# A decode block fed by one stream of transfers: two small arrays join larger transfers, one transfer is merged, one modulation moves

## The chip, the cores and the metric

The kernel runs on one NeuronCore of a Trainium2 chip. The metric is the device time in microseconds (us) of one execution. The engines are TensorE (PE: matmul, PEld: the loading of its stationary operand), VectorE (DVE), ScalarE (ACT), GpSimd (POOL) and SyncE (SP). Transfers between HBM and the on-chip memory run on 16 DMA engines, whichever engine issued them.

## The reference

All arrays are float32. Batch 2, one token, width 512; the attention has 32 heads of 128 with 4096 cached keys and values each.

```python
mod = (silu(c) @ w_mod).reshape(2, 6, 1, -1)
sa, ca, ga, sb, cb, gb = (mod[:, i] for i in range(6))
h = layernorm(x) * (1 + ca) + sa
x = x + ga * attention(h, k_cache, v_cache, wq, wo)   # q = h @ wq, softmax, @ wo
h = layernorm(x) * (1 + cb) + sb
x = x + gb * (mish(h @ w1 + b1) @ w2)                 # w1: 512 x 1376, w2: 1376 x 512
```

The keys and values are 2 x 32 x 4096 x 128 each, 134 MB each, and every byte of them is read once. A modulation is one sixth of `silu(c) @ w_mod`.

## The kernel before

**The stream.** All large inputs are laid out beforehand as rows, one for each of the 128 partitions, and are read in a fixed order that `stream()` writes out: a list of loads, each with one or more transfers. All of them are issued by SP, on one queue, at L143. Load 0 holds the weights of modulations 0 to 2 (`m012`) and the first two blocks of `wq`, in two transfers. Then come the keys and values, head by head, with blocks of `wq` and `wo` attached to some. The last three loads are the last block of `wo` with `m4` and the last head's values; `m3` with `w1` in three transfers (`m3`, the first half of `w1`, the second half); and `m5` with `w2` in five. A load goes to one of three buffers (two of tag "two", one of tag "one"), so it is issued when everything of the load three places earlier has been used (`used`, L148 to L156).

Beside the stream ACT issues three small transfers: `c` and `x` (`head`, eight rows of 512 bytes each, into `cq` and `xq`, L163 to L165) and the biases `b1c` (128 rows of 48 bytes into `bias`, L167).

**The head of the kernel.** PE turns `c` into columns (L250); silu gives `ct`. Then come the mean and the variance of the first norm (L204, L212), a matmul that puts the biases into `fps` (L263), modulations 0 to 2 (L241 under L265), the first two projections to queries (L288), all in this order on PE.

**The heads.** For each head DVE multiplies the keys by the query (L316) and sums over the 128 columns (L319); the softmax runs on ACT, and PE sums the values with the weights of an earlier head (L365).

**The tail.** After the last values, PE finishes the attention output (L403). `centred` (L194 to L213) computes mean and variance of the new `x`: PE's two matmuls (L204, L212) stand between DVE steps, and `more_work` is put between them. Modulation 3 is computed in two halves, one ahead of the mean and one ahead of the variance. Its result is used at L510, when the second norm is formed. Then follow `w1` (L521), the columns of the hidden layer on top of the biases (L536), modulation 5, mish, `w2` (L561), and the output. `busy(n)` (L293) runs matmuls whose result nobody reads, at places where PE would be idle.

Of the kernel before, what the change touches and what calls it, by code (L numbers as in the profile page):

```python
# [8 lines left out]
F32 = mybir.dt.float32  # L9
# [4 lines left out]
P = 128  # L14
WIDTHS = (384, 384, 352, 256)
# [4 lines left out]
W = 2048  # L20
SIZES = {
    "k": BIG, "v": BIG, "wq": W, "wo": W, "m012": 3 * W, "m3": W, "m4": W, "m5": W,
    "w1": 4 * sum(WIDTHS), "w2": 512 * len(CHUNKS),
}
AHEAD = (14, 22)

# [1 line left out]
def stream():  # L28

    behind, pieces = {}, [("k", 0)]
    for h in range(1, HEADS):
        pieces.append(("k", h))
        if h not in AHEAD:
            behind[h] = len(behind)
            pieces.append(("v", behind[h]))
    left = list(range(len(behind), HEADS))
    pieces += [("v", h) for h in left[:-1]]

    extra = {}
    for c in range(2, HEADS // HC):
        at = (pieces.index(("k", HC * c)) - 1) // 5 * 5
        extra[at] = [("wq", c), ("wo", c - 2)]
    extra[60] = [("wo", HEADS // HC - 2)]
    loads = [[([("m012", 0), ("wq", 0), ("wq", 1)], (3 * W, 2 * W))]]
    n = 0
    while n < len(pieces):
        m = 1 if n % 5 == 0 else 2
        keys = pieces[n : n + m]  # L50
        if keys[0] == ("v", left[0]) and m == 2:
            loads.append([([key], (BIG,)) for key in keys])
        else:
            keys = keys + (extra.pop(n, []) if m == 1 else [])
            loads.append([(keys, (sum(SIZES[kind] for kind, _ in keys),))])
        n += m
    assert not extra and len(loads) % 3 == 0
    last = HEADS - 1
    loads += [
        [([("wo", HEADS // HC - 1), ("m4", 0)], (2 * W,)), ([("v", last)], (BIG // 2, BIG // 4, BIG // 4))],  # L60
        [([("m3", 0), ("w1", 0)], (W, 2 * sum(WIDTHS), 2 * sum(WIDTHS)))],
        [([("m5", 0), ("w2", 0)], (W, 6 * 512, 3 * 512, 512, 512))],
    ]
    return loads, behind, left
# [3 lines left out]
def kernel(  # L68
# [1 line left out]
    tc: tile.TileContext,  # L70
    loads: list,
    head: bass.AP,
    b1c: bass.AP,
    behind: dict,
    left: list,
    out: bass.AP,
# [44 lines left out]
    def take(t, keys):  # L121
        lo = 0
        for kind, n in keys:
            part = t[:, lo : lo + SIZES[kind]]
            lo += SIZES[kind]
            if kind in "kv":
                (k_t if kind == "k" else v_t)[n] = part.rearrange("p (b j d) -> p b j d", b=B, d=DH)
            elif kind in ("wq", "wo"):
                (wq_t if kind == "wq" else wo_t)[n] = part.rearrange("p (k n) -> p k n", k=G)
            else:  # L130
                w_t[kind] = part.rearrange("p (k n) -> p k n", k=NCH if kind == "w2" else G)

    w_t = {}
    done = set()
# [13 lines left out]
    def used(*keys):  # L148

        nonlocal loaded  # L150
        done.update(keys)
        while loaded < len(loads) and (
            loaded < 3 or all(key in done for keys, _ in loads[loaded - 3] for key in keys)
        ):
            load(loaded)
            loaded += 1  # L156
# [1 line left out]
    used()  # L158


    cq = work.tile([P, P], F32, tag="xn", name="cq", bufs=1)
    xq = const.tile([P, P], F32, name="xq")
    for t, src in ((cq, head[0]), (xq, head[1])):  # L163
        nc.gpsimd.memset(t, 0.0)
        nc.scalar.dma_start(out=t[::TB, :], in_=src)  # L165
    bias = const.tile([P, NCH + 1], F32, name="bias")
    nc.scalar.dma_start(out=bias, in_=b1c)  # L167
    nc.scalar.preload_act_table_set("natural_log_exp_and_others")
    ident = const.tile([P, P], F32, name="ident")
    make_identity(nc, ident)  # L170
# [23 lines left out]
    def centred(src, name, first_sum=None, between=None):  # L194

        rs = const.tile([P, 8], F32, name=f"rs_{name}")
        xc = work.tile([P, P], F32, tag="xc", name=f"xc_{name}", bufs=1)
        sq = work.tile([P, P], F32, tag="sq", name=f"sq_{name}", bufs=1)
        if first_sum is None:
            nc.vector.tensor_reduce(out=rs[:, 0:1], in_=src, axis=AX.X, op=ALU.add)  # L200
        else:
            first_sum(rs[:, 0:1])
        mps = small_ps(f"mean_{name}")
        nc.tensor.matmul(mps[:, 0:1], lhsT=mean_w, rhs=rs[:, 0:1], start=True, stop=True)  # L204
        nc.vector.tensor_scalar(out=xc, in0=src, scalar1=mps[:, 0:1], scalar2=None, op0=ALU.subtract)
        nc.vector.scalar_tensor_tensor(
            sq, xc, 1.0, xc, op0=ALU.mult, op1=ALU.mult, accum_out=rs[:, 1:2]
        )
        if between is not None:
            between()  # L210
        vps = small_ps(f"var_{name}")
        nc.tensor.matmul(vps[:, 0:1], lhsT=mean_w, rhs=rs[:, 1:2], start=True, stop=True)  # L212
        return xc, vps[:, 0:1], rs  # L213
# [20 lines left out]
    def modulation(name, n, t, ps=None, ks=range(G)):  # L234


        if ps is None:
            ps = wide_ps(f"modps{name}")[:, : n * P].rearrange("p (m n) -> p m n", m=n)
        for k in ks:
            for g in range(G):  # L240
                nc.tensor.matmul(  # L241
                    ps[R * g : R * (g + 1)],
                    lhsT=ct[:, k, :],
                    rhs=t[:, k, :].rearrange("p (m n) -> p m n", m=n)[:, :, P * g : P * (g + 1)],
                    start=(k == 0),
                    stop=(k == G - 1),
                )
        return ps
# [11 lines left out]
    nc.vector.tensor_scalar(out=xn, in0=xc, scalar1=y0, scalar2=y1, op0=ALU.mult, op1=ALU.mult)  # L260

    fps = psum.tile([P, 512], F32, tag="att2", name="fps", bufs=1)[:, : NJ * G * B]
    nc.tensor.matmul(fps, lhsT=ident, rhs=bias[:, :, None].to_broadcast([P, NJ * G, B]), start=True, stop=False, skip_group_check=True)  # L263

    ps = modulation("0", 3, w_t["m012"])  # L265
    hq = const.tile([P, P], F32, name="hq")
# [1 line left out]
    nc.vector.tensor_tensor(out=hq, in0=ps[:, 0, :], in1=hq, op=ALU.add)  # L268
    mod = {}

    def keep(m, ps):
        mod[m] = const.tile([P, P], F32, name=f"mod{m}")
        nc.scalar.copy(mod[m], ps)

    keep(2, ps[:, 2, :])
    hps = columns(hq, "hps")
    hc = const.tile([P, G, B], F32, name="hc")
    nc.vector.tensor_copy(hc, hps)  # L278
# [14 lines left out]
    def busy(n):  # L293

        for lo in range(0, n, 2):
            cols = P * min(2, n - lo)
            nc.tensor.matmul(ov[1][:, :cols], lhsT=ident, rhs=e_t[0][0].rearrange("p c m -> p (c m)")[:, :cols], start=True, stop=True)
# [130 lines left out]

    project_q(0)
    project_q(1)  # L430
    used(("m012", 0), ("wq", 0), ("wq", 1))
    for h in range(H):
        products(h)
        if h:
# [61 lines left out]
    def add_x(total):  # L496
        nc.vector.scalar_tensor_tensor(x2, xg, 1.0, xq, op0=ALU.mult, op1=ALU.add, accum_out=total)

    mps3 = modulation("3", 1, wm3, ks=(0, 1))

    def more_work():
        modulation("3", 1, wm3, mps3, (2, 3))
        busy(1)

    xc, var, rs = centred(x2, "b", add_x, more_work)
    busy(6)
    nc.vector.tensor_tensor(out=m4, in0=xc, in1=m4, op=ALU.mult)
    y0, y1 = rstd(var, rs)
    nc.scalar.activation(xc, m4, AF.Copy, scale=y0)
# [37 lines left out]

    nc.vector.tensor_scalar(out=f[:, 0], in0=hid, scalar1=30.0, scalar2=None, op0=ALU.min)
    nc.scalar.activation(f[:, 0], f[:, 0], AF.Exp)
    keep(5, gps[:, 0, :])  # L550
    busy(6)
    nc.vector.scalar_tensor_tensor(f[:, 1], f[:, 0], 2.0, f[:, 0], op0=ALU.add, op1=ALU.mult)
    nc.vector.tensor_scalar(out=f[:, 2], in0=f[:, 1], scalar1=2.0, scalar2=None, op0=ALU.add)
# [20 lines left out]
def _lay_out(np, a):  # L574


    def rows(w):

        return w.reshape(-1, P, w.shape[-1]).transpose(1, 0, 2)

    def q_rows(v):

        return v.reshape(2, 4, P).transpose(1, 0, 2).reshape(8, P)

    B, H, S, DH = a["A_k_cache"].shape
    kv = {
        kind: a[n].reshape(B, H, P, -1).transpose(1, 2, 0, 3).reshape(H, P, -1)
        for kind, n in (("k", "A_k_cache"), ("v", "A_v_cache"))
    }
    wq = rows(a["A_wq"]).reshape(P, 4, 8, 512).transpose(2, 0, 1, 3).reshape(8, P, -1)  # L590
    wo = a["A_wo"].reshape(8, 4, P, 512).transpose(0, 2, 1, 3).reshape(8, P, -1)
    wm = rows(a["w_mod"])
    w1 = rows(a["B_w1"])
    starts = np.cumsum((0,) + WIDTHS)
    b1c = np.zeros((P, 12), a["B_b1"].dtype)
    w2 = np.zeros((P, len(CHUNKS), 512), a["B_w2"].dtype)
    for n, (g, j) in enumerate(CHUNKS):
        f0 = starts[g] + P * j
        f1 = min(f0 + P, starts[g + 1])
        b1c[: f1 - f0, n] = a["B_b1"][f0:f1]  # L600
        w2[: f1 - f0, n] = a["B_w2"][f0:f1]

    pieces = {**kv, "wq": wq, "wo": wo, "m012": [wm[:, :, :1536]], "w1": [w1], "w2": [w2]}
    for n in (3, 4, 5):
        pieces[f"m{n}"] = [wm[:, :, 512 * n : 512 * (n + 1)]]
    arrays = {
        "head": np.stack([q_rows(a["c"]), q_rows(a["A_x"])]),
        "b1c": b1c,
    }
    for n, parts in enumerate(stream()[0]):  # L610
        for i, (keys, widths) in enumerate(parts):
            row = np.concatenate([pieces[kind][m].reshape(P, -1) for kind, m in keys], axis=1)
            cuts = np.split(row, np.cumsum(widths)[:-1], axis=1)
            for j, t in enumerate(cuts):
                arrays[f"load{n}_{i}_{j}"] = np.ascontiguousarray(t)
    return arrays
# [24 lines left out]
```

## Time and profile before

| | us |
|---|---|
| median of three runs | 699.19 |
| lowest and highest of them | 699.03, 699.20 |
| the profiled execution, its own time | 698.83 |
| its span, first to last instruction | 697.0 |

| engine | busy us | share of the span |
|---|---|---|
| DVE | 595.8 | 85% |
| PE | 308.2 | 44% |
| ACT | 43.7 | 6% |
| POOL | 4.4 | 1% |

The span is what the trace shows; the own time holds it and 1.8 us around it. The trace moved 297.48 MB by DMA at a mean of 427 GB/s over the span. A busy share is an average over the whole span: it does not say by itself which engine sets the end.

[...]
A row of the timeline reads: start us, us, engine, line, operation, tile written and tiles read, shapes, count, and in brackets the engine's idle time before it with what ended it.

### The profile page before, as it was taken

What the parts mean: (1) busy time and instruction counts of PE and PEld (TensorE: products, weight loads), DVE (VectorE), ACT (ScalarE), POOL (GpSimd) and SP (SyncE); (2) the same over time, 40 slices, a digit from 0 to 9 for tenths busy, and PEclk for the clock granted to TensorE, in tenths of its full rate; (3) what the DMA queues carried; (4) which work ended last, traced back from release to release, by engine and by line L of the source; (5) the groups of instructions that cost most, each with busy time, mean ns of one, the idle gap of its engine ahead of it and who ended that gap; (6) DMA issues with size and microseconds to landing.
All of it is one profiled execution on the core that took longest, in us unless ns stands there. A gap on an engine that the chain in (4) does not pass through costs nothing.

```text
span 697.0 us, 4072 instructions
## 1 busy us (share of the span) xinstructions
PE 308.2 (44%) x1692; PEld 107.0 (15%) x1692; DVE 595.8 (85%) x218; ACT 43.7 (6%) x176; POOL 4.4 (1%) x22
## 2 busy tenths in 40 slices
PE   2913343523453722843034831644043832226686
PEld 1300011100110200310011200211010300002234
DVE  3399999959999769999999789999999689999501
ACT  1100000000000000010000100000000100000001
POOL 2000000000000000000000000000000000000000
PEclk9966656776556765695665865986556975666799
DMA  9999999999999999999999999999999999999996
GB/s 383 453 429 417 427 459 411 448 429 416 454 432 425 438 425 428 448 430 433 429 444 426 432 440 417 446 432 429 444 423 440 430 425 440 429 420 432 422 422 269
DMA packets 7842, 297.48 MB, mean 427 GB/s; under 512 B 1016, under 2 KB 1040, under 8 KB 1424
## 3 DMA queue, kind: packets, MB, share of 16 engines
q1 hardware_dynamic: 7648, 297.21, 98.9%
q8 instruction: 13, 0.21, 0.1%
q10 hardware_dynamic: 176, 0.01, 0.0%
q14 instruction: 5, 0.04, 0.0%
HBM read 297.22 MB, written 0.00 MB: 426 GB/s over the span
## 4 chain that ended last, share of the span: by engine, by line
DVE 72%; DMA 24%; PE 2%; issue 1%; POOL 0%; SPq 0%; ACT 0%; DVEq 0%; POOLq 0%
DVE s L319 35%; DVE two L316 25%; DMA two<-in_load 22%; DVE one L316 10%; DMA bias<-in_b1c 2%; DVE d L326 1%; PE qps L288 1%; PE modps L241 1%; DVE m L324 1%; DVE m L337 0%; DVE pick L357 0%; SPq L143 0%; DVE pick L356 0%; PE fps L263 0%; ACT q L291 0%
## 5 line engine op out<-in xcount | busy, mean ns | idle before, releaser
L316 DVE TENSOR_TENSOR two<-two,q 128x8192 f32<-128x8192 f32 x24 | 208.5, 8687 | 37.1 <-DMA two<-in_load 37.1
L319 DVE TENSOR_REDUCE s<-two 128x64 f32<-128x8192 f32 x24 | 208.2, 8675 | 0.0
L365 PE MATMUL ov<-two,e 128*32 128x512 f32 x864 | 148.0, 847 | 134.1 <-DMA two<-in_load 81.9
L331 PE MATMUL mt<-d,ones 128*128 128x256 f32 x64 | 28.6, 536 | 130.3 <-DVE d L326 130.3
L316 DVE TENSOR_TENSOR one<-one,q 128x8192 f32<-128x8192 f32 x8 | 69.5, 8685 | 7.9 <-ACT q L291 7.9
L365 PEld LDWEIGHTS ov<-two,e 128*32 128x32 f32 x864 | 33.8, 149 | 233.4 <-issue 110.3
L319 DVE TENSOR_REDUCE s<-one 128x64 f32<-128x8192 f32 x8 | 69.4, 8676 | 0.0
L339 ACT ACTIVATE e<-s,m 128x32 f32<-128x32 f32 x64 | 20.1, 314 | 483.0 <-DVE m L337 483.0
L288 PE MATMUL qps<-one,hc 128*128 128x512 f32 x96 | 45.0, 624 | 0.0
L365 PE MATMUL ov<-one,e 128*32 128x512 f32 x160 | 28.1, 867 | 32.8 <-ACT e L339 17.1
L331 PEld LDWEIGHTS mt<-d,ones 128*128 128x128 f32 x64 | 12.0, 235 | 153.5 <-DVE d L326 108.9
L348 PE MATMUL l<-l,ones 128*128 128x8 f32 (+2 forms) x18 | 5.4, 370 | 63.4 <-ACT e L339 63.4
L288 PEld LDWEIGHTS qps<-one,hc 128*128 128x128 f32 x96 | 18.9, 201 | 24.4 <-issue 24.1
L348 PEld LDWEIGHTS l<-l,ones 128*128 128x128 f32 x18 | 4.5, 312 | 68.9 <-ACT e L339 68.5
L337 DVE TENSOR_REDUCE m<-mt 128x2 f32<-128x256 f32 x32 | 13.4, 418 | 1.4 <-PE mt L331 1.4
L326 DVE TENSOR_TENSOR d<-ident,m 128x256 f32<-128x256 f32 x32 | 13.6, 425 | 1.1
L365 PEld LDWEIGHTS ov<-one,e 128*32 128x32 f32 x160 | 6.3, 154 | 52.0 <-ACT e L339 17.9
L288 PE MATMUL qps<-two,hc 128*128 128x512 f32 x32 | 14.0, 595 | 0.3 <-DVE hc L278 0.3
L387 PE MATMUL otp<-pick,o 128*128 128x8 f32 (+2 forms) x72 | 10.0, 264 | 7.6 <-DVE m L324 4.7
L291 ACT ACTIVATE q<-qps 128x512 f32<-128x512 f32 x16 | 9.4, 594 | 52.2 <-PE qps L288 52.2
L339 ACT ACTIVATION_READ_ACCUMULATOR e<-s,m 128x1 f32 x64 | 12.0, 187 | 0.0
L387 PEld LDWEIGHTS otp<-pick,o 128*128 128x128 f32 x72 | 9.2, 200 | 14.8 <-ACT o L379 9.1
(105 smaller groups left out, 95.0 us busy)
## 6 DMA issues: line engine op xcount, KB each, us to landing
one<-in_load SPq DMA_DIRECT2D x6, 6144.0 KB, 31.8
one<-in_load SPq DMA_DIRECT2D x6, 4096.0 KB, 29.7
two<-in_load SPq DMA_DIRECT2D x2, 4096.0 KB, 24.7
two<-in_load SPq DMA_DIRECT2D x3, 2048.0 KB, 14.8
one<-in_load SPq DMA_DIRECT2D x1, 5120.0 KB
two<-in_load SPq DMA_DIRECT2D x1, 3072.0 KB
two<-in_load SPq DMA_DIRECT2D x3, 1024.0 KB, 20.7
one<-in_load SPq DMA_DIRECT2D x2, 1376.0 KB
```

The source lines that it names most:

```text
L241: nc.tensor.matmul(ps[R * g : R * (g + 1)], lhsT=ct[:, k, :], rhs=t[:, k, :].rearrange("p (m n) -> p m n", m=n)[:, :, P * g : P * (g + 1)] ...
L288: nc.tensor.matmul(ps, lhsT=hc[:, k, b : b + 1].to_broadcast([P, P]), rhs=wq_t[ch][:, k, :], start=(k == 0), stop=(k == G - 1))
L291: nc.scalar.activation(q_t[ch][:, b].rearrange("p h d -> p (h d)"), ps, AF.Copy, scale=SCALE)
L316: nc.vector.tensor_tensor(out=k_t[h], in0=k_t[h], in1=qv, op=ALU.mult)
L319: nc.vector.tensor_reduce(out=s_t[h], in_=k_t[h], axis=AX.X, op=ALU.add)
L326: nc.vector.tensor_tensor(out=d, in0=ident[:, None, :].to_broadcast([P, B, P]), in1=m_t[h][:, 0:2, None].to_broadcast([P, B, P]), op=ALU.mult,
L331: nc.tensor.matmul(mps[h], lhsT=ones, rhs=d, start=True, stop=True)
L337: nc.vector.tensor_reduce(out=m[:, 2:4], in_=mps[h], axis=AX.X, op=ALU.max, negate=True)
L339: nc.scalar.activation(e_t[i][b][:, :, M * i + 4 * b : M * i + 4 * b + 4], s_t[h][:, b].rearrange("p (c m) -> p c m", m=4), AF.Exp, bias=m ...
L348: nc.tensor.matmul(lps[n][:, x], lhsT=ones, rhs=l_t[n][:, x], start=True, stop=True)
L365: nc.tensor.matmul(ov[bank][R * g : R * (g + 1), :], lhsT=e_t[h % HC][b][:, c, :], rhs=v_t[h][:, b, 4 * c : 4 * c + 4, :].rearrange("p m d ...
L387: nc.tensor.matmul(tps[:, x], lhsT=o_t[m], rhs=pick_t[n][:, m, x], start=(m == 0), stop=(m == 3),)
```

## The change

- The biases `b1` become twelve more columns behind `m012` in the rows of load 0's first transfer. `bias` and its transfer are gone; L263 reads the columns in load 0's buffer. The two blocks of `wq` in that buffer lie 48 bytes further on.
- `c` and `x` come in one transfer of eight rows of 1024 bytes, into one tile `first`, zeroed by one memset.
- `m3` and the first half of `w1` come in one transfer; the second half stays a transfer of its own.
- Modulation 3, whole, is issued on PE behind the variance's matmul and `busy(1)`. Where its halves stood, `busy(3)` and `busy(4)` stand; the `busy(6)` behind the variance is gone.
- The kept copy of modulation 5 takes the room of the tile `xc`.

```diff
-    loads = [[([("m012", 0), ("wq", 0), ("wq", 1)], (3 * W, 2 * W))]]
+    loads = [[([("m012", 0), ("b1", 0), ("wq", 0), ("wq", 1)], (3 * W + 12, 2 * W))]]
...
-        [([("m3", 0), ("w1", 0)], (W, 2 * sum(WIDTHS), 2 * sum(WIDTHS)))],
+        [([("m3", 0), ("w1", 0)], (W + 2 * sum(WIDTHS), 2 * sum(WIDTHS)))],
...
-    cq = work.tile([P, P], F32, tag="xn", name="cq", bufs=1)
-    xq = const.tile([P, P], F32, name="xq")
-    for t, src in ((cq, head[0]), (xq, head[1])):
-        nc.gpsimd.memset(t, 0.0)
-        nc.scalar.dma_start(out=t[::TB, :], in_=src)
-    bias = const.tile([P, NCH + 1], F32, name="bias")
-    nc.scalar.dma_start(out=bias, in_=b1c)
+    first = const.tile([P, 2 * P], F32, name="first")
+    nc.gpsimd.memset(first, 0.0)
+    nc.scalar.dma_start(out=first[::TB, :], in_=head)
+    cq = first[:, 0:P]
+    xq = first[:, P : 2 * P]
...
-    nc.tensor.matmul(fps, lhsT=ident, rhs=bias[:, :, None].to_broadcast([P, NJ * G, B]), start=True, stop=False, skip_group_check=True)
+    nc.tensor.matmul(fps, lhsT=ident, rhs=w_t["b1"].to_broadcast([P, NJ * G, B]), start=True, stop=False, skip_group_check=True)
...
-    mps3 = modulation("3", 1, wm3, ks=(0, 1))
-
-    def more_work():
-        modulation("3", 1, wm3, mps3, (2, 3))
-        busy(1)
-
-    xc, var, rs = centred(x2, "b", add_x, more_work)
-    busy(6)
+    busy(3)
+    xc, var, rs = centred(x2, "b", add_x, lambda: busy(4))
+    busy(1)
+    mps3 = modulation("3", 1, wm3)
...
-    keep(5, gps[:, 0, :])
+    keep(5, gps[:, 0, :], work, tag="xc", bufs=1)
```

## Rows read from the trace of the kernel before

**Rows 1.** The page: the DMA's busy tenths in 40 slices, DMA queues.

```profile
DMA  9999999999999999999999999999999999999996
...
q1 hardware_dynamic: 7648, 297.21, 98.9%
...
q10 hardware_dynamic: 176, 0.01, 0.0%
```

**Rows 2.** Busy time by stretch; the last two columns are DMA share and GB/s.

```profile
0.00:2.00 2.00, 0.00 (x0) 0.00 (x0) 0.37 (x1) 0.00 (x0) 1.40 (x11) 1.00 0.52 123
2.00:4.00 2.00, 0.00 (x0) 0.00 (x0) 1.97 (x1) 0.73 (x1) 2.00 (x10) 1.00 0.67 246
...
240.00:400.00 160.00, 73.23 (x329) 24.70 (x327) 146.17 (x45) 10.74 (x42) 0.00 (x0) 0.69 1.00 434
...
664.00:676.00 12.00, 9.45 (x106) 3.74 (x98) 0.29 (x1) 1.01 (x3) 0.00 (x0) 0.86 1.00 417
676.00:688.00 12.00, 10.87 (x140) 7.89 (x139) 3.75 (x18) 2.15 (x10) 0.42 (x1) 1.00 1.01 421
688.00:690.00 2.00, 1.23 (x6) 0.74 (x4) 0.25 (x2) 0.07 (x1) 0.00 (x0) 1.00 0.93 373
690.00:692.00 2.00, 1.71 (x56) 1.48 (x60) 0.00 (x0) 0.00 (x0) 0.00 (x0) 1.00 0.52 195
692.00:694.00 2.00, 1.31 (x40) 0.71 (x32) 0.31 (x2) 0.00 (x0) 0.00 (x0) 1.00 0.06 23
```

**Rows 3.** The chain that ended last: shares of the span by engine.

```profile
DVE 72%; DMA 24%; PE 2%; issue 1%; POOL 0%; SPq 0%; ACT 0%; DVEq 0%; POOLq 0%
```

**Rows 4.** Waits: us in total, times, longest us.

```profile
DVE two L316 <- DMA two<-in_load: 37.1, 8, 9.1
```

**Rows 5.** The timeline of the head, 0 to 32 us.

```profile
9.63 0.28 DVE L200 TENSOR_REDUCE rs_a<-xq 128x1 f32<-128x128 f32 x1 [0.22 <-DMA xq<-in_head]
...
11.37 0.56 PE L212 MATMUL var_a<-rs_a,mean_w 128*128 128x1 f32 x2 [0.81 <-DVE sq_a L206]
...
14.93 0.62 PE L263 MATMUL fps<-bias,ident 128*128 128x24 f32 x2 [3.01 <-DMA bias<-in_b1c]
...
15.48 5.35 PE L241 MATMUL modps<-two,ct 128*32 128x384 f32 x32
...
30.02 8.69 DVE L316 TENSOR_TENSOR one<-one,q 128x8192 f32<-128x8192 f32 x1 [7.85 <-ACT q L291]
```

**Rows 6.** The timeline of DVE about its first long wait.

```profile
147.51 8.69 DVE L316 TENSOR_TENSOR two<-two,q 128x8192 f32<-128x8192 f32 x1 [7.93 <-DMA two<-in_load]
```

**Rows 7.** The timeline of the tail, 676 us to the end.

```profile
678.76 0.35 PE L204 MATMUL mean_b<-rs_b,mean_w 128*128 128x1 f32 x2 [0.40 <-DVE x L497]
...
679.94 0.33 PE L212 MATMUL var_b<-rs_b,mean_w 128*128 128x1 f32 x2
...
680.13 1.54 PE L297 MATMUL ov<-e,ident 128*128 128x256 f32 x6
...
681.43 0.35 DVE L510 SCALAR_TENSOR_TENSOR hq<-xc_b,rs_b,modps 128x128 f32<-128x128 f32 x1
...
682.55 2.77 PE L521 MATMUL w1ps<-one,h2t 128*32 128x384 f32 x32
683.66 0.97 PEld L521 LDWEIGHTS w1ps<-one,h2t 128*32 128x32 f32 x16 [0.32 <-DMA one<-in_load]
...
685.89 0.83 PE L536 MATMUL fps<-ident,hq_pad 128*128 128x8 f32 x6 [0.56 <-ACT hq_pad L533]
...
688.16 0.20 DVE L556 TENSOR_TENSOR actt<-f 128x22 f32<-128x22 f32 x1
690.04 1.52 PE L561 MATMUL yps<-two,actt 128*32 128x128 f32 x48 [0.81 <-DMA two<-in_load]
...
693.09 0.42 PE L561 MATMUL yps<-two,actt 128*32 128x128 f32 x8 [0.21 <-DMA two<-in_load]
```

**Rows 8.** A stretch of the tail at the lower clock (the columns of rows 2).

```profile
670.00:672.00 2.00, 2.00 (x12) 0.39 (x8) 0.00 (x0) 0.00 (x0) 0.00 (x0) 0.50 1.02 426
```

More of the change, by code (lines that the diff above doesn't have):

```diff
@@ L22 @@
     "k": BIG, "v": BIG, "wq": W, "wo": W, "m012": 3 * W, "m3": W, "m4": W, "m5": W,
-    "w1": 4 * sum(WIDTHS), "w2": 512 * len(CHUNKS),
+    "b1": 12, "w1": 4 * sum(WIDTHS), "w2": 512 * len(CHUNKS),
 }
@@ L72 @@
     head: bass.AP,
-    b1c: bass.AP,
     behind: dict,
@@ L130, in take @@
             else:
-                w_t[kind] = part.rearrange("p (k n) -> p k n", k=NCH if kind == "w2" else G)
+                w_t[kind] = part.rearrange("p (k n) -> p k n", k={"b1": NCH + 1, "w2": NCH}.get(kind, G))
     w_t = {}
@@ L269, with keep @@
     mod = {}
-    def keep(m, ps):
-        mod[m] = const.tile([P, P], F32, name=f"mod{m}")
+    def keep(m, ps, pool, **kw):
+        mod[m] = pool.tile([P, P], F32, name=f"mod{m}", **kw)
         nc.scalar.copy(mod[m], ps)
-    keep(2, ps[:, 2, :])
+    keep(2, ps[:, 2, :], const)
     hps = columns(hq, "hps")
@@ L430 @@
     project_q(1)
-    used(("m012", 0), ("wq", 0), ("wq", 1))
+    used(("m012", 0), ("b1", 0), ("wq", 0), ("wq", 1))
     for h in range(H):
@@ L601, in _lay_out @@
         w2[: f1 - f0, n] = a["B_w2"][f0:f1]
-    pieces = {**kv, "wq": wq, "wo": wo, "m012": [wm[:, :, :1536]], "w1": [w1], "w2": [w2]}
+    pieces = {**kv, "wq": wq, "wo": wo, "m012": [wm[:, :, :1536]], "b1": [b1c], "w1": [w1], "w2": [w2]}
     for n in (3, 4, 5):
@@ L606, in _lay_out @@
     arrays = {
-        "head": np.stack([q_rows(a["c"]), q_rows(a["A_x"])]),
-        "b1c": b1c,
+        "head": np.ascontiguousarray(np.concatenate([q_rows(a["c"]), q_rows(a["A_x"])], axis=1)),
     }
```

## The prediction

> **What bounds the kernel now.** I read the page's head and DMA lines first, then the busy time by stretch, the chain of waits, DVE's waits, and at the end the timelines of the head and the tail, where the change is.
>
> The page shows a DMA line of nines from the first slice to the last but one, and one queue, SP's, that takes 98.9% of the time of all 16 DMA engines [rows 1]. The view by stretch says the same more sharply: from 240 to 400 us the DMA share is 1.00 at 434 GB/s, and it is 1.00 or 1.01 still from 664 to 688 us [rows 2]. There is no stretch in between in which a transfer was not issued in time. 297.21 MB at some 433 GB/s are 686 us, and with some 2 us before the stream is at speed and some 5 us behind its end that is nearly the whole span of 697.0 us. So the stream of transfers is the bound.
>
> The chain that ended last seems to say something else: it gives DVE 72% and DMA 24% [rows 3]. It is followed back through who released a buffer: a transfer was issued when DVE had finished with a buffer. But a transfer that is issued behind others that still run does not start any earlier for being issued earlier. DVE's own waits show who leads: eight times it waited for a transfer of keys, 37.1 us together [rows 4], the first long wait being 7.93 us ahead of 147.51 us [rows 6]. DVE had slack of 37 us; the DMA engines had none.
>
> At the end the share falls over some 4 us: 0.93, 0.52, 0.06 [rows 2]. The engines finish their parts at different times, and the last part of w2 releases PE's last eight matmuls at 693.09 us [rows 7].
>
> **The change, part by part.** The sum is made against the profiled execution: 697.0 us of span and 1.8 us around it, 698.83 us in all, 0.36 us under the median of 699.19.
>
> *Biases.* Today PE waits 3.01 us for them: the variance's matmul ends at 11.37 + 0.56 = 11.93 us, and L263 starts at 14.93 us [rows 5]. With the biases in load 0's first transfer that wait ends with this transfer. Its 3.15 MB are through at 9.6 us, an estimate from 123 GB/s up to 2 us, 246 up to 4 us and 434 from there [rows 2]; with a microsecond for the slowest engine it lands at about 10.5 us, ahead of 11.93. So modulations 0 to 2 start 3.0 us earlier, and so does the first product of keys, 27.0 instead of 30.02 us. This gains nothing at the end: DVE then reaches the keys for which it waits at 147.51 us three microseconds sooner, and waits 10.9 instead of 7.93 us [rows 6]. Buffers also come free earlier, but the engines to fill them are already busy at 1.00.
>
> *c and x.* x is used at 9.63 us after a wait of 0.22 us for its transfer [rows 5]. That 0.22 us may go; it lies in the same head, covered in the same way. The two memsets become one of both widths, ahead of the first use of c.
>
> *What the stream itself saves.* Here a gain counts in full, since every DMA engine is busy. The third queue of small transfers, c, x and biases, shows 176 packets and a share of 0.0%, so under 0.05% of 697 us, which is 0.35 us per engine [rows 1]. The stream loses the biases' transfer (128 rows of 48 bytes) and the split between m3 and w1 (another 128 rows). What do 128 more rows cost? From 664 to 688 us some eight transfers of 1 to 2 MB passed, at 417 and 421 GB/s and full share, against 434 GB/s where the rows are long [rows 2]: 24 x (1 - 419/434) = 0.83 us, or about 0.1 us a transfer. Two transfers fewer are 0.2 us. The 48 bytes a row that the biases now add are 6 KB, 0.01 us. c and x together are eight rows; joining them I put at nothing. So the stream saves 0.2 us; the bounds are nothing and 0.35 + 0.1 = 0.45 us.
>
> *Rows that no longer start evenly.* Load 0's first transfer has rows of 24624 bytes, and wq's blocks are written 48 bytes off. No row of the trace shows a large transfer with such addresses. As the lower bound it costs nothing; as the upper one I take the slowest rate at full share that the stream's trace shows, 246 / 0.67 = 367 GB/s from 2 to 4 us against 434 [rows 2]: load 0's 5.24 MB would take 14.3 instead of 12.1 us, 2.2 us more. I take nothing, because the other rows of the stream, from 2 KB to 64 KB long, all run within 4% of each other, so the price of a row is its bytes and a small fixed part. [...]
>
> *Modulation 3.* Its 32 matmuls span about 1.1 us. Before the mean and the variance stand busy matmuls instead. busy(6), three of 256 columns in 1.54 us, gives 0.51 us for each [rows 7]. busy(4), two of these, starts behind the mean's matmul (678.76 + 0.35 = 679.11 us) and ends near 680.1, so the variance moves from 679.94 to about 680.1 us. Then busy(1), 0.26 us, and modulation 3 could start at about 680.5 us. It now needs the merged transfer. The second half of w1 landed at about 683.66 us [rows 7]; it is 1.41 MB, 3.35 us at 421 GB/s, so the first half lands at 680.3 us, less the 0.2 us saved. PE does not wait, or hardly. The modulation ends at about 681.6 us, and L510, today at 681.43 us, goes at about 681.65. Everything behind moves by about 0.2 us to actt, 688.16 + 0.20 + 0.2 = 688.6 us. w2 is not there until 690.04 us: PE waited for it, having 1.6 us of slack from actt's end [rows 7]. So the shift is covered, and the last matmuls wait for the last part of w2 as before. If the cover were gone, 0.2 us would be paid.
>
> *Modulation 5's copy* takes a tile whose last reader, L510, was done 5 us before; nothing.
>
> *Sum:* -0.2 us (stream), 0 from the head, 0 from the tail: a span of 696.8 us, an own time of 698.6 us beside 698.83, and a median of 699.19 - 0.2 = **699.0 us**. A change of this kernel of less than 0.2%, 1.4 us, is about what a measurement cannot tell from none.
>
> **The rivals.**
>
> *DVE's chain carries the head's gain to the end.* For it: the chain's 72% [rows 3]. Then 3.0 us come off, and 0.2 from the stream: 696.0 us. Against it: DVE's eight waits and the full DMA share [rows 2, 4]. Chance 0.04.
>
> *Each transfer has a fixed cost in the stream.* If a transfer gave back what the stream's start costs, 123 and 246 GB/s for 2 us each against 434 [rows 2], which is 4 - 738/434 = 2.3 us, then the three transfers fewer give 6.9 us: 692.3 us. Against it stand the 0.1 us worked out above with eight transfers in 24 us at full share. [...] Chance 0.02.
>
> *The uneven rows are slow* (the other side). Load 0 at 367 GB/s costs 2.2 us: 699.0 + 2.2 = 701.2 us. All behind it is the same stream, so nothing gives it back. It decides from 1.6 us on, that is when load 0 runs 13% slower. For it: nothing in the trace has such addresses. Against it: as above. Chance 0.06.
>
> *Modulation 3 holds up the tail.* [...] It decides from a delay of 3.2 us at actt. Against it: the landing at 680.1 to 680.3 comes just ahead of PE. Chance 0.03.
>
> **How the numbers follow.** The forecast has 0.85. Around it the stream's saving may be 0 to 0.45 us, uneven rows may cost a part of the 2.2 us, runs lie 0.2 us apart, and the tail's spread of engines can differ by some tenths: 698.3 to 700.0 us holds it, and with 0.85 the other cases may be left out. Faster by over 0.2%: 0.06, the first two rivals. Slower by over 0.2%: 0.09, the last two. Within 0.2%: 0.85.
>
> **What would show it.** The DMA share stays at 1.00 up to 688 us. L263 starts near 12 us and the first L316 near 27 us; the first long wait of L316 for keys is about 3 us longer, and the sum of these waits grows from 37.1 to about 40 us. The small queue has about 40 packets. L561 still waits for w2 three times. The prediction is wrong if load 0 lands later than about 14 us plus the start, if PE waits for the merged transfer by more than a few tenths or its clock falls below 1.00 behind 676 us, or if the last L316 starts earlier with the stream's end.

## The result, and the profile after

The changed kernel takes 700.61 us (median of 22 executions) beside 699.2 us (22 of the kernel before): 1.4 us longer, ratio 1.0026, interval 1.0014 to 1.0037. Forecast were 699.0 us and a range of 698.3 to 700.0, so it lies outside, on the side that had 0.09.

The profiled execution took 700.52 us, with a span of 698.7 beside 697.0 us. First the page of the changed kernel: DMA busy tenths and the queues.

```profile
DMA  8999999999999999999999999999999999999996
...
q1 hardware_dynamic: 7504, 297.22, 98.8%
...
q10 hardware_dynamic: 16, 0.01, 0.0%
```

Against [rows 1] the small queue has lost its 160 packets and the stream 144, and yet the first slice of the span has become an 8. The changed kernel by stretch follows. A row reads, as in [rows 2] and [rows 8]: from and to in us, length, then for PE, PEld, DVE, ACT and POOL the busy us with the instructions in brackets, then the granted TensorE clock as a share of full speed, the mean busy share of the 16 DMA engines, and GB/s.

```profile
4.00:8.00 4.00, 0.00 (x0) 0.00 (x0) 0.00 (x0) 0.00 (x0) 0.57 (x3) 1.00 0.88 359
8.00:12.00 4.00, 1.45 (x6) 1.33 (x6) 1.32 (x7) 0.18 (x1) 0.00 (x0) 1.00 0.89 373
12.00:16.00 4.00, 4.00 (x28) 1.73 (x31) 0.88 (x4) 0.46 (x2) 0.00 (x0) 1.00 1.03 442
...
676.00:688.00 12.00, 10.62 (x111) 6.94 (x111) 2.86 (x13) 1.90 (x8) 0.42 (x1) 1.00 0.99 416
688.00:690.00 2.00, 2.00 (x39) 1.78 (x40) 0.84 (x5) 0.41 (x4) 0.00 (x0) 1.00 0.98 405
...
692.00:694.00 2.00, 1.73 (x65) 1.46 (x59) 0.00 (x0) 0.00 (x0) 0.00 (x0) 1.00 0.41 149
```

The same first stretches of the kernel before:

```profile
4.00:8.00 4.00, 0.12 (x1) 0.15 (x1) 0.62 (x3) 0.55 (x1) 0.54 (x3) 1.00 0.96 413
8.00:12.00 4.00, 1.59 (x6) 1.35 (x6) 1.42 (x7) 0.21 (x2) 0.00 (x0) 1.00 1.04 438
```

From 4 to 12 us, while load 0's first transfer runs, the DMA engines are no longer fully busy (0.88 and 0.89), and 359 and 373 GB/s pass instead of 413 and 438: 0.48 MB less, 1.1 us of the stream. From 12 us on the rate is nearly what it was: by the trace's records of single packets, the changed kernel has moved 0.51 MB less than the kernel before at 12 us, 0.51 MB less at 100 and 0.63 MB less at 688 us, which at 434 GB/s is 1.45 us. So the end of the stream has moved: from 692 to 694 us the share is 0.41 where it was 0.06. Nothing gives the loss back.

The head and the tail of the changed kernel in its timeline, its lines being numbered 3 to 7 lower:

```profile
12.12 0.60 PE L260 MATMUL fps<-two,ident 128*128 128x24 f32 x2
...
27.18 8.69 DVE L313 TENSOR_TENSOR one<-one,q 128x8192 f32<-128x8192 f32 x1 [7.85 <-ACT q L288]
...
682.25 1.08 PE L238 MATMUL modps<-one,ct 128*32 128x128 f32 x32
...
683.47 0.35 DVE L503 SCALAR_TENSOR_TENSOR hq<-xc_b,rs_b,modps 128x128 f32<-128x128 f32 x1 [0.47 <-PE modps L238]
...
691.64 1.52 PE L554 MATMUL yps<-two,actt 128*32 128x128 f32 x48 [0.38 <-DMA two<-in_load]
...
694.75 0.43 PE L554 MATMUL yps<-two,actt 128*32 128x128 f32 x8 [0.23 <-DMA two<-in_load]
```

The biases' matmul starts at 12.12 and the first product at 27.18 us instead of 14.93 and 30.02 [rows 5], and the last part of w2 releases PE at 694.75 instead of 693.09 us [rows 7]: 1.66 us later. The wait of the keys' product, by the view of waits:

```profile
DVE two L313 <- DMA two<-in_load: 40.9, 10, 9.3
```

### The profile page after: what moved, and what is told of

It reads as the page before. It is cut to its first block, busy times and chain, and to the rows that moved or that the text cites. A ratio compares the mean times of both kernels' runs of the same rounds, so it can differ in the third digit from the quotient of the medians.

```text
span 698.7 us, 4068 instructions
## 1 busy us (share of the span) xinstructions
PE 305.1 (44%) x1694; PEld 105.3 (15%) x1694; DVE 593.7 (85%) x218; ACT 43.4 (6%) x176; POOL 4.4 (1%) x21
## 4 chain that ended last, share of the span: by engine, by line
DVE 67%; DMA 28%; PE 3%; issue 1%; SPq 0%; ACT 0%; DVEq 0%; POOL 0%; POOLq 0%
DVE s L316 32%; DMA two<-in_load 27%; DVE two L313 23%; DVE one L313 9%; PE qps L285 2%; DVE d L323 1%; DMA first<-in_head 1%; PE modps L238 1%; DVE m L321 1%; DVE m L334 0%; DVE pick L354 0%; DVE pick L353 0%; SPq L142 0%; PE mean_a L201 0%; PE cps L228 0%
## 5 line engine op out<-in xcount | busy, mean ns | idle before, releaser
L313 DVE TENSOR_TENSOR two<-two,q 128x8192 f32<-128x8192 f32 x24 | 208.5, 8688 | 40.9 <-DMA two<-in_load 40.9
L285 PE MATMUL qps<-one,hc 128*128 128x512 f32 x96 | 42.6, 596 | 0.0
L328 PEld LDWEIGHTS mt<-d,ones 128*128 128x128 f32 x64 | 11.6, 226 | 151.6 <-DVE d L323 106.3
```

The costliest lines, as they stand in the source:

```text
L285: nc.tensor.matmul(ps, lhsT=hc[:, k, b : b + 1].to_broadcast([P, P]), rhs=wq_t[ch][:, k, :], start=(k == 0), stop=(k == G - 1))
L313: nc.vector.tensor_tensor(out=k_t[h], in0=k_t[h], in1=qv, op=ALU.mult)
L328: nc.tensor.matmul(mps[h], lhsT=ones, rhs=d, start=True, stop=True)
```

## The experiments

All were timed in five rounds (*before_24624_more_rows* and *before_wq_24624* in three) beside the kernel before on the same chip; each time is a median. The kernel before came to 699.09 to 699.29 us on these occasions, so a difference of 0.2 us says nothing by itself. Differences below are to the kernel before beside it. The ratio in brackets, with its 95% interval, is not that of the two medians: single long executions weigh in it, so that it can point the other way where the difference is small. None of the variants leaves out work; some store or read zeros that nobody uses.

**Is it the rows, the start or the tail?** Theory U: rows of 24624 bytes, which do not all start at multiples of 256 (an uneven start, below), slow load 0's first transfer. Rivals: the merged transfer of c and x disturbs the start (S); the tail's edits cost (T).

*pad_rows*, the changed kernel with

```diff
-    "b1": 12, ... (3 * W + 12, 2 * W)
+    "b1": 64, ... (3 * W + 64, 2 * W)
```

> The changed kernel with the biases padded from 12 to 64 columns, so that the rows of load 0's first transfer are 24832 bytes (97 times 256) and no row starts unevenly in HBM. Theory U (rows that start unevenly slow this transfer): the first transfer's rate comes back, the stream ends some 1.1 us or more earlier than in the changed kernel, median 699.0 to 699.4 us. Theory S (the merged transfer of c and x, or the missing bias transfer, disturbs the start): no gain, 700.6 us. Theory T (the merged m3 transfer or the moved modulation costs in the tail): 700.6 us.

699.4 us, +0.31 (ratio 1.001, 0.9996 to 1.0023). 1.1 of the 1.4 us are gone, as theory U said.

*before_dead_columns*, the kernel before with

```diff
-    loads = [[([("m012", 0), ("wq", 0), ("wq", 1)], (3 * W, 2 * W))]]
+    loads = [[([("m012", 0), ("pad", 0), ("wq", 0), ("wq", 1)], (3 * W + 12, 2 * W))]]
```

> The kernel before, with 12 columns of zeros that nobody reads behind m012 in the rows of load 0's first transfer (24624 bytes); biases, c and x, m3 and the tail as before. Theory U: load 0's first transfer takes about 1.1 us longer, median 700.3 to 700.9 us. Theories S and T: no change from before, 699.2 us.

700.22 us, +1.13 (1.0009, 1.0 to 1.0019). Twelve columns that nobody reads cost most of what the change costs, 0.1 us less than theory U gave at the least.

*own_bias*, the changed kernel with

```diff
-    loads = [[([("m012", 0), ("b1", 0), ("wq", 0), ("wq", 1)], (3 * W + 12, 2 * W))]]
+    loads = [[([("m012", 0), ("wq", 0), ("wq", 1)], (3 * W, 2 * W))]]
...
+    nc.scalar.dma_start(out=bias, in_=b1c)
```

> The changed kernel with the biases in a transfer of their own again; c and x in one, m3 merged and modulation 3 moved. Theory U: 699.0 to 699.3 us, as the rows of load 0 are even again. Theories S (by c and x) and T: it stays near 700.6 us.

698.75 us, -0.34 (0.9993, 0.9984 to 1.0003). That is 0.25 us below theory U's range. All the other parts of the change together cost nothing; S and T fall.

*bias_second*, the changed kernel with

```diff
-([("m012", 0), ("b1", 0), ("wq", 0), ("wq", 1)], (3 * W + 12, 2 * W))
+([("m012", 0), ("wq", 0), ("wq", 1), ("b1", 0)], (3 * W, 2 * W + 12))
```

> The changed kernel with the biases at the end of load 0's second transfer, behind the two blocks of wq: its rows are 16432 bytes, the first transfer's 24576. Theory U, whatever the place in the stream: the second transfer (4.9 us) slows by the same 13%, some 0.6 us, so 699.6 to 699.9 us. If uneven rows cost only in the first transfer, while the engines get going: 699.0 to 699.3 us. Theories S and T: 700.6 us.

699.4 us, +0.31 (1.0009, 0.9995 to 1.0023), with 432 and 419 GB/s from 4 to 12 us and 476 from 12 to 16: rows of 16432 bytes, as uneven, do not slow their transfer. The time lies between the two that theory U gave; where the 0.3 us come from is told below.

**Start or length, first transfer or any?**

*far_rows*, the changed kernel, whose host side adds 52 columns to that array, and

```diff
+    args["loads"][0][0][1][0] = args["loads"][0][0][1][0][:, : 3 * W + 12]
```

> The changed kernel with load 0's first transfer stored in HBM 24832 bytes a row, of which 24624 are read: the rows start at multiples of 256, their length stays uneven. If the uneven start costs: the transfer's rate comes back, 699.2 to 699.5 us, as with padded rows that were read whole. If the uneven length costs: it stays at 700.4 to 700.8 us.

699.29 us, +0.19 (1.0003, 0.9995 to 1.0012). The time is in the range for the uneven start: the length is innocent, and so are the 48 bytes by which wq's blocks lie further on.

*before_near_rows*, the kernel before, whose host side adds 12 columns to that array, and

```diff
+    args["loads"][0][0][1][0] = args["loads"][0][0][1][0][:, : 3 * W]
```

> The kernel before, with m012's rows stored 24624 bytes apart, of which 24576 are read as before: uneven start, even length, every byte and tile on the chip as before. If the uneven start costs: as with the dead columns, 700.1 to 700.4 us. If the uneven length costs: 699.1 us, as before.

700.09 us, +0.99 (1.0015, 1.0006 to 1.0025). Every byte that is moved, and every place on the chip, is as before; only the distance of the rows in HBM, and with it the array's size, has changed. Its stretches:

```profile
4.00:8.00 4.00, 0.00 (x0) 0.00 (x0) 0.60 (x3) 0.54 (x1) 0.52 (x3) 1.00 0.95 389
8.00:12.00 4.00, 1.28 (x5) 1.16 (x6) 1.42 (x7) 0.18 (x1) 0.00 (x0) 1.00 0.87 358
```

*uneven_behind*, the changed kernel with

```diff
-([("m012", 0), ("b1", 0), ("wq", 0), ("wq", 1)], (3 * W + 12, 2 * W))
+([("wq", 0), ("wq", 1), ("m012", 0), ("b1", 0)], (2 * W, 3 * W + 12))
```

> The changed kernel with load 0's two transfers the other way round: wq's even rows of 16384 bytes first, then m012 with the biases in uneven rows of 24624 bytes. If uneven rows cost only in the stream's first transfer, while the engines get going: 699.2 to 699.6 us. If they cost at any place: 700.4 to 700.8 us, and the rate falls by some 13% from about 7 to 15 us instead of from 4 to 12 us.

700.46 us, +1.36 (1.0018, 1.0009 to 1.0027). The loss moves with the transfer, to the stretches from 8 to 16 us (the execution profiled took 706.3 us; what made it long lies in its tail, as the last section shows):

```profile
4.00:8.00 4.00, 0.56 (x2) 0.50 (x2) 0.00 (x0) 0.05 (x1) 0.56 (x3) 1.00 1.11 475
8.00:12.00 4.00, 1.14 (x4) 1.00 (x4) 1.77 (x10) 0.59 (x3) 0.00 (x0) 1.00 0.94 400
12.00:16.00 4.00, 0.00 (x0) 0.00 (x0) 0.43 (x2) 0.00 (x0) 0.00 (x0) 1.00 0.76 320
```

*mid_rows*, the kernel before with

```diff
-            loads.append([(keys, (sum(SIZES[kind] for kind, _ in keys),))])
+            dead = 12 if len(keys) == 3 else 0
+            loads.append([(keys, (sum(SIZES[kind] for kind, _ in keys) + dead,))])
```

> The kernel before, with 12 dead columns behind each of the six transfers of rows of 49152 bytes in the middle of the stream (keys or values with wq and wo): six transfers of uneven rows, 14.5 us each. If uneven rows slow a transfer by 13% at any place: six times 1.9 us more, about 710 us. If only the stream's first transfer suffers: 699.1 to 699.4 us, as the 37 KB more are 0.1 us.

699.05 us, -0.05 (0.9998, 0.9989 to 1.0006). Six transfers of uneven rows in the middle cost nothing that can be told. So it is neither the first place in the stream nor unevenness anywhere, and both readings that I had set against each other fall.

**Which distance of the rows?** All are *before_near_rows* with another number of columns added (16, 76 and 8), read as there.

```diff
-np.zeros((P, 12), t.dtype)
+np.zeros((P, 16), t.dtype)
```

> The kernel before with m012's rows stored 24640 bytes apart (385 times 64, no multiple of 128 or 256), of which 24576 are read. If a start at a multiple of 64 is enough: 699.1 us. If it takes a multiple of 256: 699.9 to 700.3 us, as with 24624.

699.07 us, -0.22 (1.0004, 0.9995 to 1.0013).

> The kernel before with m012's rows stored 24880 bytes apart (24832 + 48), of which 24576 are read. The rows start at the same remainders of 256 as with 24624. If the uneven start as such costs in this transfer: 699.9 to 700.3 us. If 24624 is a pitch that suits badly by itself: 699.1 us.

699.04 us, -0.25 (0.9997, 0.9988 to 1.0005). These rows start at the same remainders of 256 as those that cost 1 us. The theory of the uneven start falls. The first stretches run as before:

```profile
4.00:8.00 4.00, 0.29 (x2) 0.32 (x2) 0.60 (x3) 0.54 (x1) 0.52 (x3) 1.00 0.96 413
8.00:12.00 4.00, 1.42 (x6) 1.18 (x5) 1.42 (x7) 0.37 (x2) 0.00 (x0) 1.00 1.03 436
```

> The kernel before with m012's rows stored 24608 bytes apart, 24576 of each read. 24640, 24832 and 24880 bytes apart cost nothing, 24624 costs 1.0 us. If the cost comes with a start at no multiple of 64 close to a pitch of 24576: 699.9 to 700.3 us. If it is of 24624 alone: 699.1 us.

699.13 us, -0.09 (0.9998, 0.9989 to 1.0006).

*before_rows_24624_late* puts the zeros ahead of the rows' bytes:

```diff
-np.concatenate([t, np.zeros((P, 12), t.dtype)], axis=1)   ...   [:, : 3 * W]
+np.concatenate([np.zeros((P, 12), t.dtype), t], axis=1)   ...   [:, 12:]
```

> The kernel before with m012's rows 24624 bytes apart, and of each the last 24576 bytes read instead of the first: the pitch that costs, with every row's start 48 bytes on. If the pitch costs: 699.9 to 700.3 us. If the cost hangs on where the rows start: another time, 699.1 us at the least.

700.06 us, +0.84 (1.0013, 1.0004 to 1.0022).

*before_24624_more_rows*, *before_near_rows* with

```diff
+t = np.concatenate([t, np.zeros((40, 3 * W + 12), t.dtype)], axis=0)
```

> The kernel before with m012's rows 24624 bytes apart in an array of 168 rows in HBM, of which 128 are read; the array is 0.98 MB longer, so that arrays may lie elsewhere. If the pitch of the rows costs: 699.9 to 700.3 us. If the cost came with the array's size or its neighbours' place: 699.1 us.

700.02 us, +0.92 (1.0014, 1.0004 to 1.0023). It is the distance, not this one size of the array.

*before_wq_24624*, the kernel before with wq's array widened instead:

```diff
+np.zeros((P, 6156 - 2 * W), t.dtype)   ...   args["loads"][0][0][1][1][:, : 2 * W]
```

> The kernel before with the rows of load 0's second transfer, wq's 16384 bytes, stored 24624 bytes apart, and m012's 24576 apart as before. If the pitch costs whatever the array: the second transfer loses rate from 8 to 14 us, and the median is 699.5 to 700.2 us. If it hangs on the length read or on this array: 699.1 us.

699.32 us, +0.22 (1.0, 0.9986 to 1.0013), with 414, 427 and 430 GB/s from 4 to 16 us. The same distance costs nothing that can be told where only 16384 bytes of each row are read.

The traces' records of single rows agree with the medians. Wherever m012's transfer came first, its rows began at 1.8 us; the last of them ended at 11.6 to 11.7 us in the six traces with a distance of 24624, and at 10.4 to 11.0 us in the other thirteen. The rows themselves took little longer: 1016 ns in the mean in *before_near_rows* beside 996 before, which is 0.16 us for the eight rows that each DMA engine moves. Most of the 1 us is time in which the engines moved nothing, as the DMA share says: from 4 to 12 us it was 0.91 instead of 1.00.

**What is left: the buffers' place.** With good rows (*far_rows*, *pad_rows*, *bias_second*) the biases in the stream still cost 0.2 to 0.3 us, where the tail's and head's savings should show. Without `bias`, and with mod5 in the room of `xc`, the stream's buffers start at byte 48672 of a partition instead of 48736, that is 32 instead of 96 bytes behind a multiple of 256. These places are added up from the sizes of the tiles; no row of a trace shows an address. *own_bias* keeps `bias`, and with it the place of before.

*far_rows_64* and *far_rows_224* are *far_rows* with a tile of 16 and of 56 columns (64 and 224 bytes) that nobody uses:

```diff
+    const.tile([P, 16], F32, name="gap")
     first = const.tile([P, 2 * P], F32, name="first")
```

> The changed kernel with its rows stored 24832 bytes apart, and 64 bytes left free ahead of the tile of c and x, so that the stream's buffers lie where they lay before (in the changed kernel and its variants with the biases in the stream they lie 64 bytes lower). Theory A (the remaining 0.2 to 0.3 us of these variants over before come from the buffers' place): the 64 KB rows, which took 1.1 ns more each, fall back, and the median is 698.7 to 699.0 us. Theory B (they come from somewhere else, as the earlier start of PE and DVE): 699.3 us, as without the gap.

698.99 us, -0.30 (1.0007, 0.9992 to 1.0021). The median is in theory A's range, but the interval reaches to both sides, so that the rows of the table below have to decide.

> The same with 224 bytes left free, so that the three buffers of the stream start at multiples of 256 bytes. Theory A: at most as long as with 64 bytes free, 698.2 to 699.0 us. Theory B: 699.3 us.

696.89 us, -2.40 (0.9969, 0.9957 to 0.9981; five executions), outside what either theory gave: below A's range.

*before_256* and *after_256* are the kernels before and after with such a gap of 40 and 56 columns.

> The kernel before with 160 bytes left free, so that its buffers start at multiples of 256; nothing of the change. If the buffers' place is worth 2 us by itself: 697.0 to 697.3 us. The difference to 696.9 us is then what the rest of the change is worth with rows that are stored well, forecast as 0.2 us by fewer transfers.

697.21 us, -2.01 (0.9975, 0.9964 to 0.9986; seven executions). The buffers' place is worth 2 us by itself.

> The changed kernel as it is (rows of 24624 bytes, 24624 apart) with 224 bytes left free, so that the stream's buffers start at multiples of 256. If the 24624 bytes cost on the reading side: 1.1 us over the kernel with the same gap and rows 24832 apart (696.9 us), so 698.0 us. If they cost only together with the buffers' uneven place: 696.9 us.

698.35 us, -0.87 (0.9993, 0.9976 to 1.0009): 1.46 us over *far_rows_224*, timed on another occasion, so the rows' distance costs no less with well placed buffers; forecast were 1.1 us over it.

The trace's records of single rows show where most of these 2 us lie. Mean ns that a row of so many bytes took:

```
                     past 256        8192    32768    65536 bytes
before               96             314.3   1217.4   2422.9
after, far_rows      32             315.8   1218.1   2423.9
far_rows_64          96             314.9   1216.6   2423.0
before_256           at 0           309.0   1213.8   2419.5
far_rows_224         at 0           310.2   1213.3   2419.6
```

(For after and far_rows the first of the two is given; they differ by 0.1.) A row of these lengths costs 3 to 6 ns more at the two uneven places than where the buffers start at a multiple of 256; rows of 2 KB cost 1.2 ns more (85.2 beside 84.0). All the rows of the stream together, over 16 engines, took 689.1 us before and 687.6 in *before_256*: 1.5 of the 2.0 us. Where the other 0.5 us lie the records do not say. Between the two uneven places it is 0.35 us (*far_rows* 689.45, *far_rows_64* 689.10). No other place was tried, so whether a multiple of 64 or 128 would do as well as one of 256 is open.

## Why the prediction was wrong

*The bound was right.* The DMA engines set the end, with a share of 0.99 from 676 to 688 us: what the stream lost in its first 12 us (0.51 MB) was still missing at 688 us (0.63 MB), and what its rows gained with well placed buffers (1.5 us of the 2.0 by the records) came off the end.

*The head was right.* L263's matmul was forecast at 12 us and came at 12.12; the first product at 27.0 and came at 27.18; the waits for keys at about 40 us and came at 40.9. The three microseconds went into these waits, and the rival that carried them to the end was wrong. It was closer than it looked: load 0's first transfer was to land at about 10.5 us, 1.4 us ahead of its use, and by the records it landed at 11.6.

*The tail was right.* PE waited for no transfer at modulation 3, and actt's chain stayed ahead of w2: 0.38 us of wait are left of 0.81. L503's own delay was larger than the 0.2 us forecast: it waited 0.47 us for the modulation. The *own_bias* run has this tail and is not slower than before.

*The stream's saving fits, as far as it can be told.* Forecast were 0.2 us for two transfers fewer. *own_bias*, which has the biases' transfer still, came to -0.34 us with an interval that holds no change, and *far_rows_224* to 0.32 us under *before_256*, on another occasion. Both are near what can be told. The rival of a fixed cost of 2 us and more for each transfer falls with them. The small queue was forecast at about 40 packets and has 16.

*The failed step is the part on rows that no longer start evenly: "I take nothing".* It measured 0.8 to 1.5 us: 1.2 in the changed kernel, 700.61 (+1.41) against *far_rows* (+0.19); +0.99 by itself in *before_near_rows*; 1.46 between *after_256* and *far_rows_224*. Its upper bound, 2.2 us, held it, and the third rival had the right transfer and the right side, with a price twice too high and a chance of 0.06. My reason for nothing was that rows from 2 to 64 KB run within 4% of each other; but all of these lay at the distance of their own length, and none at 24624. The reading was also wrong for the short ones: the 2 KB rows of the kernel before took 85.2 ns each, 385 GB/s on 16 engines beside 433 for the 64 KB rows (2422.9 ns), 11% less; the stretches had averaged over them. Nor is it the uneven start: at distances of 24608 and 24880 bytes uneven starts cost nothing that can be told (699.13 and 699.04 us beside 699.22 and 699.29), nor did they in the rows of 49200 bytes of *mid_rows* (699.05 us beside 699.10), and the rows of 16432 bytes of *bias_second* passed at 419 and 476 GB/s from 8 to 16 us. What costs is the distance of 24624 bytes between m012's rows, whichever 24576 bytes of each are read (+0.99 us with the first, +0.84 with the last). Why this distance and not its neighbours is open: the records show only that the engines moved nothing for part of the time (a share of 0.91 from 4 to 12 us in *before_near_rows*, 1.00 before). With 16384 bytes of each row read, in wq's array, it did not show (699.32 us, +0.22).

*A term was missing: the place of the buffers.* That a tile of 48 bytes that goes, and another that moves, shift the stream's buffers by 64 bytes was not in my list of what the change moves. It costs 0.35 us by the records of the rows, and 0.5 by the medians of *far_rows* (+0.19) and *far_rows_64* (-0.30), which by themselves tell no difference. So the sum is, to the kernel before: -0.34 for the other parts, some 0.4 for the place and 1.2 for the rows' distance: about +1.3 of the 1.4 us measured.

*The fastest version* is the changed kernel with rows stored 24832 bytes apart and buffers at multiples of 256: 696.89 us, 3.7 us under the changed kernel and 2.4 under the one before. 2.0 of the 2.4 us are to be had without the change, and whether the rest is a gain is not settled: 7 of the 108 executions of the changed kernel and its variants took some 5.6 us more than their median, 0.36 us in the mean of all, and none of those of the kernel before and its variants did.

## What to carry to other kernels

Where the DMA engines are busy throughout, count what a change does to every row of the stream: where the rows start on the chip, how far apart they lie in HBM, and how many there are; here 3 to 6 ns a row were worth 1.5 us at the end, and the 3 us that PE and DVE saved in the head nothing. A small array that joins a larger one changes the distance of all the larger one's rows (here from 24576 to 24624 bytes, 1.2 us), and a small tile that goes away moves the tiles behind it (here by 64 bytes, 0.35 us by the records). Check the rate in the stretch of the transfer that was widened before looking at the place that the change was meant for.

## What the hardware showed that was not expected

A row's time went with the place where its buffer starts on the chip, as the table shows: a row of 64 KB took 3.4 ns more at 96 bytes past a multiple of 256 than at one (2422.9 beside 2419.5), and 4.4 ns more at 32 bytes past (2423.9). Why the place counts, the records do not say.

One distance of rows in HBM, 24624 bytes, took 12 to 16% off the rate from 4 to 12 us (426 GB/s before, 360 to 374 in the runs with it), and 24608, 24640, 24832 and 24880 did not (423 to 428 GB/s).

Two of the 22 executions of the changed kernel took 706.2 and 706.3 us. The profiled execution of *uneven_behind* was as long, 706.3 us, and shows a granted clock of 0.50 in its tail; the kernel before had 0.50 too, from 670 to 672 us [rows 8], but 1.00 from 676 us on. Its stretches:

```profile
676.00:678.00 2.00, 1.73 (x8) 0.16 (x8) 0.00 (x0) 0.00 (x0) 0.00 (x0) 0.60 1.06 451
684.00:686.00 2.00, 2.00 (x7) 1.64 (x7) 0.65 (x4) 0.02 (x1) 0.00 (x0) 0.50 1.06 444
692.00:694.00 2.00, 2.00 (x21) 1.20 (x15) 0.00 (x0) 0.00 (x0) 0.00 (x0) 0.63 0.34 129
```

and two rows of its timeline:

```profile
690.14 4.40 PE L514 MATMUL w1ps<-one,h2t 128*32 128x384 f32 x32
...
698.37 2.61 PE L554 MATMUL yps<-two,actt 128*32 128x128 f32 x88
```

PE had waited 1.00, 0.56 and 1.43 us for the last values when its granted clock fell to 0.50 at about 676.4 us; it rose again at about 693.5 (worked out from the means of 0.60 and 0.63 in the first and the last of these stretches). Modulation 3 waited for no transfer, but took 1.94 instead of 1.08 us, w1 4.40 instead of 2.77 us, and w2's matmuls, which otherwise wait for w2, started at 698.37 us without waiting. In the trace of the changed kernel the waits are nearly the same (0.62, 0.56 and 1.42 us) and the clock stays at 1.00 there, so what makes it fall in some executions is open. *own_bias*, with the same tail, had no such execution in eleven, which at 7 in 108 says little.
